# The attention rows x are written to DRAM from Pool's DMA queue instead of SyncE's

## The chip, the cores and the metric

The kernel runs on one core of a Trainium2 chip. The metric is device time in microseconds of one execution. Of the kernel before there are three timed runs (1334.05, 1337.35 and 1341.32 us, median 1337.35) and one execution taken with the hardware profiler (1334.38 us, of which 1332.6 us lie between the first and the last instruction).

## The reference

Three steps, all in float32, on 8 x 576 = 4608 tokens:

1. Chunked attention: q, k, v of 8 batches, 8 heads, 576 positions, 64 dimensions. In each chunk of 64 positions the softmax of the scaled scores weights v. The heads of a token are put side by side, so x has 4608 rows of 512.
2. A mixture of experts with a skip: tokens with x @ w_skip > 0 go to the one of 8 experts with the largest logit x @ w_gate, and get x + p * relu(x @ w1[e]) @ w2[e], where p is that expert's softmax weight. Other tokens keep x.
3. A dense layer: h = x @ w_in (512 to 2048), an activation made of three quadratic and linear pieces, and then @ w_out (back to 512).

## The kernel before, in words

**Tiling.** The 4608 tokens are cut into 18 units of 256 (UNIT, NU), each of two halves of 128. A unit's q, k and v are 512 KB each. The loop at line 849 is software-pipelined over units: iteration i transposes q and k of unit i+2 (s_T, e_T), loads q and k of unit i+4 and v of unit i+2 (load_qk, load_v), transposes the exponentials of unit i (s_ET), takes the scores of unit i+1 (s_SC), the weighted sum of unit i (s_AV), the transposes of x of unit i-1 (s_XT), the logits of unit i-2 (s_LG), its choice of expert (s_SEL), and the ranks of unit i-3 (s_RANK), which end in two scatters of token numbers into the experts' lists (f_put, line 578).

**The rows x.** s_AV writes a unit's rows into the tile xn: line 382 clears the last four columns on Pool, line 400 multiplies the sums by the reciprocals on VectorE, once for each half. The pool of xn has 4 buffers, so the tile of unit u is taken again by unit u+4. Some iterations later f_gate (line 497) puts the token's gate weight into column 512 with a reciprocal (line 500), and calls put_x, which writes the 256 rows of 516 floats to x_dram. For the last two units the columns 0 to 511 are written earlier, straight after s_AV (lines 876 and 902), and f_gate writes columns 512 to 515 alone.

**The order around the write.** All instructions of the attention part are issued in the order in which the program lists them (tc.manual_schedule). Small VectorE steps wait in the list `fill`; a call of dve() emits the next one between larger steps. The nine steps of s_SEL(u), f_gate the last of them, are emitted in iteration u+3, f_gate between the two halves of s_AV. In that iteration SyncE's queue has the loads of q and k (line 266, two to four DMAs), the eight loads of v (line 280), and then the write of unit u (line 507). Pool has the memset of line 382 and the two scatters. An engine takes its instructions in order, and a DMA that must wait for data holds back those behind it on the same engine.

**After attention.** The last iterations also load and split the weights of the first expert (piece; the low parts by VectorE or Pool, line 166) and run an early block of tokens (s_EARLY, b_X to b_M2). Then, from about 256 us, the experts, and from about 515 us the dense layer, which are bound by matmuls. Experts gather rows of x_dram by index, from Pool.

Of the kernel before, what the change touches and what calls it, by code (L numbers as in the profile page):

```python
# [86 lines left out]
def kernel(ctx, tc, q, k, v, w_skip, w_gate, w1, w2, w_in, w_out, consts, out):  # L87
    nc = tc.nc
# [363 lines left out]
    def e_SEL(us, b):  # L452
# [44 lines left out]
        def f_gate():  # L497
            T["gated", us[0]] = True
            for i, (u, xn) in enumerate(zip(us, xs)):
                nc.vector.reciprocal(out=xn[:, :, GATE:GATE + 1], in_=sm[:, 2 * i:2 * i + 2])  # L500
                put_x(u, xn, slice(DM if u + 2 >= NU else 0, ROW))
# [2 lines left out]

    def put_x(u, xn, cut):
        rows = x_dram[u * UNIT:(u + 1) * UNIT, cut].rearrange("(s p) c -> p s c", p=P)
        (nc.sync if cut.start == 0 else nc.scalar).dma_start(out=rows, in_=xn[:, :, cut])

    scat, hots = [], []

# [293 lines left out]
    with tc.manual_schedule():  # L804
# [44 lines left out]
        for i in range(NU - 1):  # L849
# [25 lines left out]
            if i + 2 == NU:  # L875
                put_x(i, T["x", i], slice(0, DM))
# [23 lines left out]
        run(b[:2])  # L900
        s_AV(u, 1)
        put_x(u, T["x", u], slice(0, DM))
        b_X()
        q = s_RANK(u - 3)
# [36 lines left out]
        for s in range(4):  # L941
# [3 lines left out]
            out=key, in0=cnt, scalar=float(NE), in1=cst[:, C_PREF - C_SEL:C_PREF - C_SEL + NE], op0=ALU.mult, op1=ALU.add  # L945
# [7 lines left out]
            out=perm, in0=cst[r24, C_POS - C_SEL:C_POS - C_SEL + NL], scalar=own[r24, 1:2], in1=cst[r24, C_BLK - C_SEL:C_BLK - C_SEL + NL], op0=ALU.is_equal, op1=ALU.mult  # L953
# [42 lines left out]
    with tc.If(total > 0):  # L996
        fb = tc.tile_pool(name="fb", bufs=1, reuse_waits="tile")
        with fb as f_p, tc.For_i(0, NE, 1) as j:
# [4 lines left out]
            with tc.For_i(0, n_j, 1) as b:  # L1003
# [8 lines left out]
                    out=fx, out_offset=None, in_=x_dram[:, :], in_offset=bass.IndirectOffsetOnAxis(ap=fi[:, 0:1], axis=0)  # L1012
# [5 lines left out]
                for h in range(4):  # L1018
                    w = f_p.tile([P, KD, 2 * P], F32, tag="fw", name="fw", bufs=3)
                    nc.sync.dma_start(  # L1020
                        out=w, in_=w1.rearrange("e (k p) f -> p (e k) f", p=P)[:, bass.ds(e * KD, KD), h * 2 * P:(h + 1) * 2 * P]
# [7 lines left out]
                for h in range(4):  # L1029
                    w = f_p.tile([P, 2, DM], F32, tag="fw", name="fw", bufs=3)  # L1030
                    nc.sync.dma_start(
                        out=w, in_=w2.rearrange("e (f p) d -> p (e f) d", p=P)[:, bass.ds(e * (F1 // P) + 2 * h, 2), :]
# [5 lines left out]
                    out=fx[:, 0:DM], in0=bk, scalar=fx[:, GATE:GATE + 1], in1=fx[:, 0:DM], op0=ALU.mult, op1=ALU.add  # L1038
                )
                nc.gpsimd.indirect_dma_start(  # L1040
                    out=x_dram[:, :],
                    out_offset=bass.IndirectOffsetOnAxis(ap=fi[:, 0:1], axis=0),
                    in_=fx,
# [238 lines left out]
```

## Time and profile before

| | |
|---|---|
| Median of the timed runs | 1337.35 us |
| The profiled execution: its time, its span | 1334.38 us, 1332.6 us |
| TensorE busy (matmuls) | 1252.7 us, 94% |
| VectorE, ScalarE, Pool busy | 678.6, 663.1, 216.5 us |
| DMA queue q1, issued by SyncE | 136.24 MB |
| DMA queue q10, issued by ScalarE | 46.75 MB |
| DMA queue q0, software, issued by Pool | 18.70 MB |

Busy time of TensorE is an average over stages. The page's second part shows the span in 40 slices of 33 us: each digit is the busy share of a slice in tenths, and PEclk the granted clock in tenths of full speed (2.4 GHz; the other level is 1.2). A wait is idle time of an engine just before an instruction, put down to what ended last by the profile. "issue" is time for which the profile shows no cause. In the list of DMA queues, the share is of the time of the core's 16 DMA engines.

### The profile page before, as it was taken

How to read it: one execution, taken by the hardware profiler on the slowest of the kernel's cores; microseconds unless marked ns; L12 is line 12 of the kernel's file. 1: busy time of each engine (PE TensorE's matmuls, PEld its weight loads, DVE VectorE, ACT ScalarE, POOL GpSimd, SP SyncE). 2: the span in 40 equal slices, each digit the busy share in tenths (PEclk: the TensorE clock that was granted, in tenths of full speed). 3: DMA queues.
4: the chain of work that ended last, by engine and by line, in shares of the span. 5: the costliest groups of instructions: out<-in, count | busy, mean ns of one | idle time of the engine just before them, and what ended most of it. 6: DMA issues, size and time to landing. Idle time of an engine off the chain costs nothing.

```text
span 1332.6 us, 19838 instructions
## 1 busy us (share of the span) xinstructions
PE 1252.7 (94%) x7127; PEld 1056.2 (79%) x7128; DVE 678.6 (51%) x1308; ACT 663.1 (50%) x1115; POOL 216.5 (16%) x259
## 2 busy tenths in 40 slices
PE   7877867889989999999999999999999999999998
PEld 6766856679878987888888888887888888888887
DVE  6645647647777675211221121001866686668665
ACT  7756645235544421222332232223776687668764
POOL 3011115532443444011111111000000000000000
PEclk9989888799999999999999999999999999999999
DMA  9879797267667666433543432234443343334431
GB/s 219 205 144 156 161 146 195 89 190 266 225 219 252 192 206 213 165 131 138 171 153 110 159 140 108 109 118 150 121 125 118 113 126 119 119 121 117 126 118 41
DMA packets 165371, 202.98 MB, mean 152 GB/s; under 512 B 51274, under 2 KB 88421, under 8 KB 165270
## 3 DMA queue, kind: packets, MB, share of 16 engines
q1 hardware_dynamic: 130966, 136.24, 38.1%
q10 hardware_dynamic: 26320, 46.75, 9.3%
q0 software_dynamic: 7984, 18.70, 4.4%
q8 instruction: 57, 0.93, 0.3%
q14 instruction: 44, 0.36, 0.1%
HBM read 135.88 MB, written 66.48 MB: 152 GB/s over the span
## 4 chain that ended last, share of the span: by engine, by line
PE 72%; DVE 3%; DMA 2%; issue 1%; ACT 0%; POOL 0%; SPq 0%; ACTq 0%; DVEq 0%; POOLq 0%
PE b L137 30%; PE a L137 29%; PE bank L137 6%; PE big L137 5%; PE t L140 1%; DMA stg<-in_moe_w_dram 1%; DVE a L192 1%; DVE a L191 1%; DMA stg<-in_moe_w_in_dram 0%; DVE s L193 0%; PE t L137 0%; PE big L687 0%; DVE hl L716 0%; DVE al L166 0%; DMA xs<-x_dram 0%
## 5 line engine op out<-in xcount | busy, mean ns | idle before, releaser
L137 PE MATMUL b<-bh,xh 128*128 128x512 f32 x576 | 226.0, 392 | 1.7 <-ACT xh L1181 1.7
L137 PE MATMUL b<-bh,xl 128*128 128x512 f32 x576 | 225.7, 392 | 0.0
L137 PE MATMUL b<-bl,xh 128*128 128x512 f32 x576 | 224.8, 390 | 0.0
L137 PE MATMUL a<-xh,ah 128*128 128x512 f32 (+1 forms) x576 | 223.9, 389 | 0.0
L137 PE MATMUL a<-xl,ah 128*128 128x512 f32 (+1 forms) x576 | 222.6, 386 | 0.4 <-DVE xl L1135 0.3
L137 PE MATMUL a<-xh,al 128*128 128x512 f32 (+1 forms) x576 | 222.5, 386 | 0.0
L1159 ACT COPY hs<-a 128x512 f32<-128x512 f32 x142 | 83.3, 587 | 275.6 <-PE a L137 264.9
L1182 DVE TENSOR_TENSOR xl<-r,xh 128x512 fp32r<-128x512 f32 x144 | 99.7, 692 | 108.7 <-ACT xh L1181 97.5
L1135 DVE TENSOR_TENSOR xl<-t,xh 128x512 fp32r<-128x512 f32 x34 | 22.0, 687 | 230.4 <-ACT xh L1134 230.3
L137 PEld LDWEIGHTS b<-bh,xh 128*128 128x128 f32 x576 | 108.4, 188 | 26.9 <-ACT xh L1181 5.0
L137 PEld LDWEIGHTS b<-bh,xl 128*128 128x128 f32 x576 | 108.5, 188 | 26.3 <-DVE xl L1182 3.9
L137 PEld LDWEIGHTS b<-bl,xh 128*128 128x128 f32 x576 | 108.6, 188 | 22.5
L137 PEld LDWEIGHTS a<-xl,ah 128*128 128x128 f32 x576 | 108.3, 188 | 22.0 <-DVE xl L1135 0.8
L137 PEld LDWEIGHTS a<-xh,al 128*128 128x128 f32 x576 | 108.2, 188 | 22.0
L137 PEld LDWEIGHTS a<-xh,ah 128*128 128x128 f32 x576 | 108.2, 188 | 21.5 <-ACT xh L1134 0.3
L1171 DVE SCALAR_TENSOR_TENSOR hs<-hs,r 128x512 f32<-128x512 f32 x144 | 99.7, 692 | 46.0 <-ACT r L1170 46.0
L1181 ACT CAST xh<-r 128x512 fp32r<-128x512 f32 x144 | 89.6, 622 | 53.3 <-PE b L137 34.5
L1175 ACT ACTIVATE hs<-hs,bias 128x512 f32<-128x512 f32 x144 | 104.2, 723 | 0.4 <-ACT hs L1159 0.4
L1170 ACT ACTIVATE r<-hs,bias 128x512 f32<-128x512 f32 x144 | 102.1, 709 | 0.5 <-ACT hs L1159 0.5
L1176 DVE TENSOR_TENSOR r<-r,hs 128x512 f32<-128x512 f32 x144 | 99.7, 693 | 2.6 <-ACT hs L1175 2.0
L326 ACT COPY qt<-big 64x512 f32<-64x512 f32 x72 | 44.7, 621 | 62.4 <-PE big L140 61.6
L140 PE MATMUL big<-ident,qu 128*128 128x128 f32 x144 | 26.8, 347 | 45.9 <-issue 40.2
(217 smaller groups left out, 2041.7 us busy)
## 6 DMA issues: line engine op xcount, KB each, us to landing
h_dram<-hs ACTq DMA_DIRECT2D x144, 256.0 KB
hs<-h_dram SPq DMA_DIRECT2D x144, 256.0 KB
stg<-in_moe_w_dram SPq DMA_DIRECT2D x128, 256.0 KB
vbd<-in_v_dram SPq DMA_DIRECT2D x144, 64.0 KB
xs<-x_dram SPq DMA_DIRECT2D x17, 512.0 KB
out_dram<-o ACTq DMA_DIRECT2D x34, 256.0 KB
x_dram<-xn SPq DMA_DIRECT2D x16, 516.0 KB
stg<-in_moe_w_in_dram SPq DMA_DIRECT2D x16, 512.0 KB
```

Source lines behind the costliest of these rows:

```text
L137: nc.tensor.matmul(out=o, lhsT=l, rhs=r, start=start, stop=stop)
L140: nc.tensor.transpose(out=o, in_=i, identity=ident)
L191: nc.vector.tensor_scalar(out=a, in0=top, scalar1=3, scalar2=0x3FFFFFFF, op0=ALU.logical_shift_left, op1=ALU.bitwise_and)
L326: (nc.vector.tensor_copy if eng is nc.vector else nc.scalar.copy)(out=o, in_=b4[64 * r:64 * r + 64, :, par, :])
L1135: nc.vector.tensor_tensor(out=xl[:, :, cut], in0=b3, in1=xh[:, :, cut], op=ALU.subtract)
L1159: nc.scalar.copy(out=hs, in_=b)
L1170: nc.scalar.activation(out=r, in_=h, func=ACTF.Relu, bias=bias[:, 0:1])
L1171: nc.vector.scalar_tensor_tensor(out=h, in0=h, scalar=-1.0, in1=r, op0=ALU.max, op1=ALU.subtract)
L1175: nc.scalar.activation(out=h, in_=h, func=ACTF.Square, scale=0.5, bias=bias[:, 1:2])
L1176: nc.vector.tensor_tensor(out=r, in0=r, in1=h, op=ALU.add)
L1181: nc.scalar.copy(out=gh, in_=r)
L1182: nc.vector.tensor_tensor(out=gl, in0=r, in1=gh, op=ALU.subtract)
```

## The change

put_x issues its DMA on Pool (nc.gpsimd) where it issued it on SyncE (nc.sync). The condition is not changed: it holds where the columns start at 0.

```
     def put_x(u, xn, cut):
         rows = x_dram[u * UNIT:(u + 1) * UNIT, cut].rearrange("(s p) c -> p s c", p=P)
-        (nc.sync if cut.start == 0 else nc.scalar).dma_start(out=rows, in_=xn[:, :, cut])
+        (nc.gpsimd if cut.start == 0 else nc.scalar).dma_start(out=rows, in_=xn[:, :, cut])
```

Its three calls:

```
put_x(u, xn, slice(DM if u + 2 >= NU else 0, ROW))   # f_gate, every unit
put_x(i, T["x", i], slice(0, DM))                    # line 876, i = NU - 2
put_x(u, T["x", u], slice(0, DM))                    # line 902, u = NU - 1
```

## Rows read from the trace of the kernel before

**Rows 1.** The page, parts 1 and 2: TensorE's busy time, and its slices.

```profile
PE 1252.7 (94%) x7127; PEld 1056.2 (79%) x7128; DVE 678.6 (51%) x1308; ACT 663.1 (50%) x1115; POOL 216.5 (16%) x259
...
PE   7877867889989999999999999999999999999998
```

**Rows 2.** Busy time by stretch: us, each engine, clock, DMA share, GB/s.

```profile
0.00:20.00 20.00, 13.21 (x120) 11.89 (x121) 11.23 (x17) 13.06 (x22) 11.77 (x31) 1.00 0.98 247
20.00:57.00 37.00, 35.55 (x455) 31.30 (x456) 26.38 (x73) 33.81 (x58) 0.00 (x0) 1.00 0.82 191
57.00:201.00 144.00, 103.17 (x1129) 92.97 (x1129) 71.35 (x274) 79.86 (x141) 20.85 (x31) 0.86 0.83 156
```

**Rows 3.** VectorE in order of time, lines 400 and 500: start, us, instruction, idle before.

```profile
39.60 0.69 DVE L400 TENSOR_TENSOR xn<-big,rc 128x512 f32<-128x512 f32 x1
...
48.46 0.69 DVE L400 TENSOR_TENSOR xn<-big,rc 128x512 f32<-128x512 f32 x1
...
106.10 0.16 DVE L500 RECIPROCAL xn<-sm 128x2 f32<-128x2 f32 x1
...
118.15 0.69 DVE L400 TENSOR_TENSOR xn<-big,rc 128x512 f32<-128x512 f32 x1 [3.49 <-DMA x_dram<-xn]
...
118.83 0.16 DVE L500 RECIPROCAL xn<-sm 128x2 f32<-128x2 f32 x1
...
134.82 0.69 DVE L400 TENSOR_TENSOR xn<-big,rc 128x512 f32<-128x512 f32 x1
...
145.86 0.69 DVE L400 TENSOR_TENSOR xn<-big,rc 128x512 f32<-128x512 f32 x1
...
201.18 0.69 DVE L400 TENSOR_TENSOR xn<-big,rc 128x512 f32<-128x512 f32 x1
```

**Rows 4.** Waits, 57 to 201 us: total us, times, longest.

```profile
POOL xn L382 <- DMA x_dram<-xn: 132.3, 10, 49.3
...
DVE xn L400 <- DMA x_dram<-xn: 41.1, 10, 6.0
PE big L140 <- issue: 40.2, 10, 6.0
```

**Rows 5.** SyncE's DMA issues in order of time.

```profile
33.25 0.55 SPq L266 DMA_DIRECT2D qu<-in_q_dram  x1
...
41.28 1.14 SPq L266 DMA_DIRECT2D qu<-in_q_dram  x2
...
109.63 0.55 SPq L507 DMA_DIRECT2D x_dram<-xn  x1
```

**Rows 6.** TensorE in order of time: eight transposes of q.

```profile
48.39 1.07 PE L140 MATMUL big<-ident,qu 128*128 128x128 f32 x8
...
134.57 1.94 PE L140 MATMUL big<-ident,qu 128*128 128x128 f32 x8 [5.44 <-issue]
```

**Rows 7.** DMA: the stretch 57 to 201 us, then the whole page's.

```profile
DMA packets 49028, 22.41 MB, mean 156 GB/s; under 512 B 25718, under 2 KB 46198, under 8 KB 49014
...
q0 software_dynamic: 640, 0.01, 0.4%
...
q0 software_dynamic: 7984, 18.70, 4.4%
...
x_dram<-xn SPq DMA_DIRECT2D x16, 516.0 KB
```

**Rows 8.** Pool: L207 by tile, L578 by line (57 to 201 us), L382 in time.

```profile
L207 POOL DMA_DIRECT2D m2w<-stg x8: 760/772/791, 321.1 to 461.7; - x8
...
L578 POOL DMA_INDIRECT idx_dram<-cst,si x20 | 19.7, 985 | 31.7 <-DVE acc L555 28.6 <-issue 3.0
...
118.19 0.10 POOL L382 MEMSET xn<- 128x8 f32 x1 [7.83 <-DMA x_dram<-xn]
```

**Rows 9.** Pool in order of time, in the tail of attention.

```profile
223.37 2.49 POOL L166 TENSOR_TENSOR al<-stg,ah 128x512 fp32r<-128x512 f32 x2 [4.43 <-ACT ah L164]
```

## The prediction

> **What bounds the kernel now.** I read the page first: TensorE is busy for 94% of the span [rows 1], so time can only come from slices in which it is not. Those are the first ten, up to the end of attention; from about 300 us on nearly every digit is 9. The view by stretches narrows it [rows 2]: from 20 to 57 us TensorE works 35.55 of 37 us at a granted clock of 1.00; from 57 to 201 us only 103.17 of 144 us, at a mean clock of 0.86, while ScalarE, VectorE and Pool have slack too (79.86, 71.35 and 20.85 us). The DMA engines show the same share in both stretches (0.82 and 0.83) but move 191 GB/s in the first and 156 GB/s in the second.
>
> What begins at 57 us? The second xn multiply of each unit (line 400) is a good clock for the loop [rows 3]. Unit 2 to unit 3 takes 48.46 - 39.60 = 8.86 us. From unit 3 (48.46) to unit 14 (201.18) there are eleven units in 152.7 us, 13.88 us each. The waits [rows 4] say why: VectorE stands 41.1 us in ten waits at line 400, Pool 132.3 us at the memset of line 382, both for the DMA x_dram<-xn. There are four xn buffers, so unit u+4 may not be written until the rows of unit u have left. TensorE's 40.2 us of "issue" in ten pieces are the same ten stalls one step on: its next transposes need a PSUM buffer that the multiply has not yet freed.
>
> The transfer itself is not long; it stands in a queue [rows 5]. Unit 4's gate is written at 106.10 [rows 3]. SyncE, which still issues loads of v, comes to the write at 109.63. Memset and multiply of unit 8 start at 118.19 and 118.15 [rows 3, 8]: freed 8.6 us after issue, 12.1 us after the gate. The next gate follows that multiply by 0.7 us (118.83) [rows 3], so the loop cannot be shorter than 12.1 + 0.7 = 12.8 us; from gate to gate this period was 118.83 - 106.10 = 12.7 us. So the write's lag is the loop's length.
>
> The eleven units add up: 8.86 of work x 11 = 97.5; waits 41.1; the remaining 14.1 us is mostly clock. After a stall eight transposes span 1.94 us where they otherwise span 1.07 [rows 6]; with 24 transposes a unit that is up to 3 x 0.87 = 2.6 us. Unit 10, which had no wait but began in this state, took 145.86 - 134.82 = 11.04 us [rows 3, 6].
>
> **The change part by part.** *Which writes move.* The condition is cut.start == 0. It is true also of the columns 0 to 511 of the last two units (lines 876 and 902), so all 18 large writes leave SyncE's queue, the 16 of 516 KB [rows 7] and those two; only the two small writes of the last units' gates stay on ScalarE's.
>
> *SyncE* loses 11 issues of about 0.55 us in the stretch, and more important, its loads are no longer issued behind a write, nor the write behind loads. Without writes it issued a unit's loads in 41.28 - 33.25 = 8.0 us [rows 5], which fits under 8.86.
>
> *Pool* gains 18 issues. A write of 512 KB from Pool took 0.77 us (L207, eight times); the two index scatters of a unit take 0.99 us each [rows 8]. Per unit Pool then has 0.77 + 2 x 0.99 + 0.10 = 2.9 us of a period of 9 to 14: hidden. In Pool's order the write stands after the unit's memset, and waits for the reciprocal of line 500. Behind it are the two scatters, whose index VectorE makes only after the gate, and the next unit's memset, which is not wanted before the next multiply. Nothing there is late by more than the 0.77 us.
>
> *The write's lag.* It would be issued at its gate, at 106.1 instead of 109.6. The trace of before shows no such write from Pool, so I bound issue-to-free: not below the 2.5 us or so that the bytes need at the highest rate of rows 2 (0.53 MB at 247 GB/s is 2.1, and some issue), not above today's 8.6 us unless Pool's queue is served worse (a rival below). With 8.6 the write allows a loop of 0.8 + 8.6 + 0.7 = 10.1 us, with 2.5 one of 4.0 us. Either way it is shorter than the next limit, so ten waits of 41.1 us go.
>
> *What is late next: the DMA engines.* In the stretch 22.41 MB move, 2.04 MB a unit [rows 7]. The bytes stay. From below: compute alone, 8.86 us a unit (it would need 230 GB/s; 247 were reached at the start). From above: today's 156 GB/s, 13.1 us. Between: 2.04 MB at the 191 GB/s of the undisturbed stretch is 10.7 us; and the time the engines are busy now, 0.83 x 13.1 = 10.9 us a unit, at the 0.98 share of the first stretch is 11.1 us [rows 2]. I take 11.0 us. Gain: 11 x (13.88 - 11.0) = 31.7 us. Bounds: 11 x (13.88 - 8.86) = 55 us, and 11 x (13.88 - 13.1) = 9 us.
>
> The Trainium skill, page "DMA: Bandwidth & Descriptors", section "Issuing engines are not separate DMA queues", says that DMAs from any issuing engine run on the same 16 DMA engines and that spreading them saves only issue time. By that rule alone the bytes would go no faster, and the time would be that of the first rival below. The rows agree as far as the equal share goes (0.82, 0.83), but the wait in rows 4 is for one write's place in line, not for bytes.
>
> *After 201 us.* Unit 15 (11.1 us, no wait) begins at the low clock and may gain 1 to 2 us. In the tail Pool splits weights (L166) between waits for ScalarE, one of 4.43 us [rows 9]. Five of the writes fall there (units 13 to 17): hidden in such waits they cost nothing, uncovered 5 x 0.77 = 3.9 us; I take 1.5. The two cancel. Everything from 256 us on shifts.
>
> **The sum** against the profiled execution: its own time is 1334.38 (span 1332.6). 1334.4 - 31.7 = 1302.7. The median before, 1337.35, lies 3.0 us above that execution: 1305.7, so I say **1305**.
>
> **Rivals.**
> *The DMA engines are full already (0.17).* The waits then turn into waits of the transposes for q and k, or of the matmuls of s_AV for v. For it: share 0.83 all through, and a rate that fell when the writes began. Against: a 17% rest, and ten waits that all name the write and none that name a load. At 13.1 us a unit the gain is 9 us, at 13.5 it is 4: about 1331.
> *Compute is the next limit (0.15).* For it: 247 GB/s in the first 20 us. Against: that stretch has no writes. 55 us: 1282.
> *Pool's queue serves the write worse (0.10): slower.* The place is the same wait at lines 382 and 400. It decides when gate-to-free plus 0.7 us exceeds 13.9, that is when issue-to-free exceeds 12.4 us instead of 8.6. At 14 us the loop is 15.5 us: 11 x 1.6 = 18 us more, 1355. For it: Pool has to generate this transfer itself and its queue moved only 0.01 MB in the stretch [rows 7]. Against: L578 beside the same VectorE work takes 0.99 us as everywhere.
> The Trainium skill, page "SBUF — State Buffer", section "SBUF: two separate sides", warns that a DMA issued from Pool stalls while a two-port VectorE instruction holds the shared port. By it the lag would grow by the length of such an instruction, 0.69 us if it is as long as line 400's, a fifth of what this rival needs; no row shows it.
> *The change does less than it says (0.03).* If only the writes inside the loop mattered and the last two units stayed, the result would differ by under 1.6 us: no case of its own.
>
> **How the numbers follow.** Forecast (10 to 12.5 us a unit, gain 15 to 43) 0.55; compute limit 0.15; engines full 0.17; slower 0.10; the rest 0.03. I put the eight-in-ten range from the compute limit to the engines-full case: 1281 to 1333. About 0.5% (6.7 us) is what a measurement of this kernel can tell from no change. Faster: 0.55 + 0.15 + 0.10 of the engines-full case + 0.01 of the rest = 0.81; same: 0.07 of the engines-full case + 0.01 of the slower one + 0.02 of the rest = 0.10; slower 0.09.
>
> **What would show it.** Right: line 400's wait for x_dram<-xn falls from 41.1 us to under 10; unit 14's second multiply comes near 170 instead of 201; clock of the stretch above 0.9; the software queue carries some 9.5 MB more than its 18.70; 18 Pool issues of line 507 near 0.8 us; after attention the same times, shifted. The DMA step is right if waits for qu, ku or vbd appear and units take 10 to 12 us; wrong if units take 9 us (then the engines were not the next limit) or stay at 13. The whole is wrong if line 382 still waits for x_dram<-xn as long as now.

## The result: faster by 1.4%, less than forecast

The changed kernel takes 1320.28 us in the median of four runs, the one before 1339.34 beside it: a ratio of 0.986, with a 95% interval of 0.982 to 0.990. The forecast was 1305 us, a gain of 32 us; the gain is 19 us, and 12.2 us between the two profiled executions (spans 1332.6 and 1320.4 us). The measured time lies inside the range of 1281 to 1333 us.

The profile after, busy time by stretch (us, then TensorE, its weight loads, VectorE, ScalarE and Pool, the granted clock, the DMA share and GB/s), is to be read against [rows 2]:

```profile
20.00:57.00 37.00, 33.33 (x432) 29.29 (x430) 25.05 (x68) 31.73 (x54) 0.88 (x2) 1.00 0.81 196
57.00:201.00 144.00, 115.01 (x1310) 101.23 (x1308) 86.34 (x327) 92.44 (x166) 36.22 (x49) 0.89 0.79 170
```

TensorE works 12 us more in the same 144 us, and the rate goes from 156 to 170 GB/s at a share of the DMA engines that is lower than before, 0.79 against 0.83. So the engines were not what filled up.

The waits of that stretch (total us, times, longest), against [rows 4]:

```profile
POOL xn L382 <- DMA x_dram<-xn: 25.4, 6, 10.1
...
PE big L137 <- DMA vbd<-in_v_dram: 11.5, 5, 4.8
...
PE big L140 <- DMA qu<-in_q_dram: 7.7, 3, 6.5
PE big L140 <- DMA ku<-in_k_dram: 7.0, 3, 4.4
...
DVE xn L400 <- DMA x_dram<-xn: 2.9, 2, 2.6
```

Line 400's wait for the row write falls from 41.1 to 2.9 us. In its place stand waits for loads: 11.5 + 7.7 + 7.0 = 26.2 us of TensorE. The first of these kinds, TensorE's wait for v, was not in the profile of before at all.

The second multiply of units 3, 14, 15 and 17 in the changed kernel, VectorE in order of time, against [rows 3]:

```profile
50.22 0.69 DVE L400 TENSOR_TENSOR xn<-big,rc 128x512 f32<-128x512 f32 x1
...
177.25 0.69 DVE L400 TENSOR_TENSOR xn<-big,rc 128x512 f32<-128x512 f32 x1
...
196.75 0.69 DVE L400 TENSOR_TENSOR xn<-big,rc 128x512 f32<-128x512 f32 x1
...
220.42 0.69 DVE L400 TENSOR_TENSOR xn<-big,rc 128x512 f32<-128x512 f32 x1
```

The kernel before had units 15 and 17 here:

```profile
212.30 0.69 DVE L400 TENSOR_TENSOR xn<-big,rc 128x512 f32<-128x512 f32 x1
...
235.02 0.69 DVE L400 TENSOR_TENSOR xn<-big,rc 128x512 f32<-128x512 f32 x1
```

Eleven units take 177.25 - 50.22 = 127.0 us, 11.55 each instead of 13.88. At unit 14 the changed kernel is 201.18 - 177.25 = 23.9 us ahead; at unit 15 only 15.6, at unit 17 14.6, at the end 12.2. A third of the gain is lost in one unit. There TensorE waits for the last load of q, which SyncE had issued 13.5 us earlier (SyncE's issue, then TensorE's transposes):

```profile
171.31 0.38 SPq L266 DMA_DIRECT2D qu<-in_q_dram  x1
```
```profile
184.82 1.94 PE L140 MATMUL big<-ident,qu 128*128 128x128 f32 x8 [6.55 <-DMA qu<-in_q_dram]
```

Pool's issues and its queue, against [rows 7, 8]: 18 writes at 0.76 us each, and 28.20 MB where there were 18.70.

```profile
L507 POOL DMA_DIRECT2D x_dram<-xn x18: 718/764/792, 50.3 to 233.0; - x18
```
```profile
q0 software_dynamic: 10576, 28.20, 6.4%
```

### The profile page after: what moved, and what is told of

It reads as the page before. It is cut to its first block, busy times and chain, and to the rows that moved or that the text cites. A ratio compares the mean times of both kernels' runs of the same rounds, so it can differ in the third digit from the quotient of the medians.

```text
span 1320.4 us, 19843 instructions
## 1 busy us (share of the span) xinstructions
PE 1244.3 (94%) x7126; PEld 1047.5 (79%) x7128; DVE 681.9 (52%) x1308; ACT 663.0 (50%) x1115; POOL 230.5 (17%) x277
## 3 DMA queue, kind: packets, MB, share of 16 engines
q0 software_dynamic: 10576, 28.20, 6.4%
## 4 chain that ended last, share of the span: by engine, by line
PE 74%; DVE 3%; DMA 1%; issue 1%; ACT 0%; SPq 0%; ACTq 0%; DVEq 0%
PE b L137 30%; PE a L137 29%; PE bank L137 6%; PE big L137 6%; PE t L140 1%; DVE a L192 1%; DVE a L191 1%; DMA stg<-in_moe_w_dram 1%; DMA stg<-in_moe_w_in_dram 1%; PE t L137 0%; PE big L687 0%; DVE s L193 0%; DVE al L166 0%; DMA xs<-x_dram 0%; PE spare L137 0%
## 5 line engine op out<-in xcount | busy, mean ns | idle before, releaser
L137 PEld LDWEIGHTS a<-xh,ah 128*128 128x128 f32 x576 | 108.2, 188 | 21.5 <-ACT xh L1134 0.3
L204 POOL TENSOR_TENSOR a<-a,bh 128x512 f32<-128x512 f32 x16 | 20.7, 1292 | 267.3 <-ACT bh L203 267.3
```

The costliest lines, as they stand in the source:

```text
L137: nc.tensor.matmul(out=o, lhsT=l, rhs=r, start=start, stop=stop)
L204: nc.gpsimd.tensor_tensor(out=af, in0=af, in1=hi, op=ALU.subtract)
```

## The experiments

My first theory: the row write's lag in SyncE's queue, against four buffers, was the loop's length, and any way of shortening it brings the gain. The first three runs undo or replace one part of that; the fourth looks at what stalls the loads. "us a unit" below is always from the second multiply of unit 3 to that of unit 14, divided by eleven, from one profiled execution. It says how long the loop is, not the whole time: in the profiles of runs 1, 2 and 9 the eleven units take 10.7, 12.9 and 14.7 us less than before, but unit 17 is then only 1.4, 8.7 and 4.3 us ahead. Each ratio is against runs of the kernel before beside that run.

**1. A fifth buffer, writes still on SyncE.**

```
-        et = e_p.tile([P, 2, HP, P], F32, tag="et", name="et")
+        et = e_p.tile([P, 2, HP, P], F32, tag="et", name="et", bufs=1)
...
-            T["x", u] = x_p.tile([P, 2, ROW], F32, tag="xn", name="xn", bufs=4)
+            T["x", u] = x_p.tile([P, 2, ROW], F32, tag="xn", name="xn", bufs=5)
```

> The kernel before, its writes still on SyncE, with a fifth xn buffer (paid for by one et buffer instead of two). My theory (the wait is one write's lag in SyncE's queue against four buffers): the unit u+5 instead of u+4 waits for the write, so the wait of line 400 for x_dram<-xn falls from 41 us to under 8, and the time falls by about as much as with Pool's queue, 12 to 20 us. Rival (the queue itself matters, because loads behind a write are held up): the wait goes but waits for q, k and v take its place, gain under 6 us.

Ratio 0.998 (0.996 to 1.001): no gain, at 12.91 us a unit. Its waits, 57 to 201 us:

```profile
DVE xn L400 <- DMA x_dram<-xn: 19.8, 7, 5.7
PE big L140 <- DMA qu<-in_q_dram: 10.4, 4, 5.2
PE big L140 <- DMA ku<-in_k_dram: 6.1, 4, 2.2
PE big L137 <- DMA vbd<-in_v_dram: 5.0, 4, 2.1
```

The wait for the write is halved, and 21.5 us of waits for loads take its place. This is the rival's outcome: the loop gets shorter, the time does not. What the single et buffer costs by itself no run shows.

**2. The writes on ScalarE's queue.**

```
-        (nc.sync if cut.start == 0 else nc.scalar).dma_start(out=rows, in_=xn[:, :, cut])
+        nc.scalar.dma_start(out=rows, in_=xn[:, :, cut])
```

> All writes of x on ScalarE's queue instead of Pool's. My theory (any queue apart from the loads does it): within 5 us of the changed kernel, some 15 us under the one before; line 400's wait for x_dram<-xn under 8 us. Rival (there is something in Pool's software queue, good or bad): more than 8 us off the changed kernel, either way.

Ratio 0.999 (0.998 to 1.001), 12.71 us a unit. Line 400 waits for no write any more, but v is late:

```profile
PE big L137 <- DMA vbd<-in_v_dram: 18.4, 10, 3.7
```

My theory falls here: a queue apart from the loads is not enough. Nor is a place ahead of the scatters, which the write has here too: ScalarE issues it at 107.36, the scatters of the unit before follow at 109.17 (below). And ScalarE is hardly held up by its new work: its instruction behind the write waits 2.0 us in all for VectorE.

```profile
107.36 0.37 ACTq L507 DMA_DIRECT2D x_dram<-xn  x1
```
```profile
ACT xt L418 <- DVE sl L562: 2.0, 2, 1.2
```

The Trainium skill, page "DMA: Bandwidth & Descriptors", section "Issuing engines are not separate DMA queues", says that another issuing engine saves only issue time. This run agrees with it (0.999), the changed kernel (0.986) does not.

The same run shows what the loads wait for. Pool issues two index scatters:

```profile
109.17 0.98 POOL L578 DMA_INDIRECT idx_dram<-cst,si  x1 [6.53 <-DVE acc L555]
110.45 0.98 POOL L578 DMA_INDIRECT idx_dram<-cst,si  x1 [0.30 <-issue]
```

and this is what all DMA moves around them, in stretches of 2 us (the last two columns are the DMA share and GB/s):

```profile
109.00:111.00 2.00, 1.03 (x5) 1.06 (x6) 0.33 (x3) 0.00 (x0) 1.53 (x2) 0.70 1.16 334
111.00:113.00 2.00, 2.00 (x12) 1.94 (x11) 0.00 (x0) 0.99 (x2) 0.43 (x1) 0.50 1.05 258
113.00:115.00 2.00, 2.00 (x21) 1.42 (x21) 0.61 (x1) 1.95 (x4) 0.00 (x0) 0.95 0.30 29
115.00:117.00 2.00, 2.00 (x34) 1.79 (x32) 1.34 (x6) 1.95 (x5) 0.10 (x1) 1.00 0.27 15
117.00:119.00 2.00, 1.27 (x17) 1.02 (x16) 2.00 (x8) 1.75 (x5) 0.00 (x0) 1.00 0.12 26
119.00:121.00 2.00, 0.00 (x0) 0.00 (x0) 0.94 (x4) 0.48 (x1) 0.00 (x0) 1.00 0.28 49
```

For 8 us next to nothing moves, 15 to 49 GB/s, though loads of v are queued, and the DMA engines are mostly without a packet (a share of 0.12 to 0.30). This is the longest such stretch of the run's loop. In others the share stays high while the rate falls (1.25 at 42 GB/s in the changed kernel, shown further down).

**3. The loads listed behind the write, on SyncE.**

```
-            load_qk(i + 4)
-            load_v(i + 2)
             s_ET(i)
...
             s_AV(i, 1)
+            load_qk(i + 4)
+            load_v(i + 2)
```

> The writes stay on SyncE, but each unit's loads are listed behind the unit's write instead of ahead of it. My theory (place in line): the write is issued within 1 us of its gate where SyncE is not late, the lag falls from 12 us to 6 to 9, the wait of 41 us to under 20, the time by 5 to 15 us. Rival (a write ahead of loads in one queue costs the loads what it saves itself): no change within 5 us.

Ratio 0.997 (0.994 to 0.999), 13.44 us a unit; line 400 still waits 25.9 us for the write. A place ahead in line takes 15 us off that wait and hardly shows in the time: no change within 5 us, as the rival had it.

**4. The changed kernel without the scatters of units 0 to 11.**

```
         def f_put():
+            if u < NU - LATE:
+                return
```

> The changed kernel without the index scatters of units 0 to 11 (left out; the lists of these units stay at their first values, so the tokens gathered are other ones). In the changed kernel the loads stall after about 65 us: slices of 1 us fall to 29 to 70 GB/s with the engines busy. Theory A (the stalls come from the scattered 4-byte index writes): the stalls go, units take 9 to 9.5 us instead of 11.5, unit 14 ends near 155 instead of 177, the time falls by another 15 to 25 us. Theory B (they come from the row writes beside loads): the time stays within 5 us of the changed kernel.

1284.59 us, ratio 0.965 (0.961 to 0.968) against the kernel before. Its stretch:

```profile
57.00:201.00 144.00, 128.37 (x1525) 109.42 (x1523) 107.42 (x408) 103.50 (x191) 36.36 (x50) 0.94 0.77 211
```

211 GB/s at a smaller share than before the change, and 8.95 us a unit, close to the 8.86 that [rows 3] show for compute alone. This is theory A: the scatters cost the stretch nearly everything above compute.

**5. As many small writes, 64 bytes apart.** far_dram is a tensor of its own that nothing reads.

```
+    far_dram = tc.dram_tile([(NE * NT + P) * 16, 1], F32, name="far_dram")
...
-            ... scalar1=FAR, scalar2=None, op0=ALU.add)
+            ... scalar1=FAR, scalar2=float(16), op0=ALU.add, op1=ALU.mult)
...
-                    out=idx_dram[:, :],
+                    out=far_dram[:, :],
...
-                    bounds_check=NE * NT - 1,
+                    bounds_check=(NE * NT - 1) * 16,
```

> The changed kernel with each scattered index written to a slot 64 bytes from the next instead of 4 (in a tensor of its own that nobody reads, so the lists keep their first values and other tokens are gathered, as in the run without scatters). As many 4-byte writes as before. Theory A1 (the stall comes from many small writes close together in memory): stalls mostly go, unit 14 under 155 us, time within 8 us of the run without scatters (1285). Theory A2 (each small write costs the same wherever it lands): time within 6 us of the changed kernel (about 1320).

1278.13 us, ratio 0.960 (0.955 to 0.966); 8.98 us a unit:

```profile
57.00:201.00 144.00, 128.89 (x1532) 109.83 (x1531) 109.86 (x412) 104.45 (x192) 60.97 (x74) 0.93 0.78 212
```

So it is not the number of the small writes but how close they lie: in the kernel before, neighbouring tokens of one expert take neighbouring slots, 4 bytes apart. The page "DMA: Bandwidth & Descriptors" of the Trainium skill, section "Specifications", says that below 512 bytes the DMA reads, modifies and writes. That would hold at either distance; the runs show that with 64 bytes between them the same writes cost the loop nothing that can be seen.

**6. The slots 16 bytes apart, read and used.** The lists are four times as long, set by four DMAs, and read with a stride (excerpts):

```
-    idx_dram = tc.dram_tile([NE * NT + P, 1], F32, name="idx_dram")
+    idx_dram = tc.dram_tile([(NE * NT + P) * 4, 1], F32, name="idx_dram")
+    idx_w = idx_dram.rearrange("(n w) o -> n (w o)", w=4)
...
-        il = dec_p.tile([NL, P], F32, tag="a", name="il")
+        il = dec_p.tile([NL, P * 4], F32, tag="a", name="il")
...
-        mm(bk[:, 0:NL], il, perm)
+        mm(bk[:, 0:NL], il.rearrange("b (p w) -> b p w", w=4)[:, :, 0], perm)
```

> The changed kernel with list slots 16 bytes apart, read and used (four times the bytes to set and to read the lists). By A1 a part of the stalls goes: 1295 to 1315. By A2: 1320 to 1326, a little above the changed kernel for the longer first setting of the lists.

1283.25 us, ratio 0.964 (0.958 to 0.969): better than I expected by 12 us, and better than both kernels of this study. 9.14 us a unit. In the 2 us stretches around two of its scatters (issued at 95.89 and 97.20) the rate does not break down; the lowest is 131 GB/s:

```profile
97.00:99.00 2.00, 2.00 (x28) 1.42 (x28) 0.94 (x3) 1.95 (x4) 1.09 (x2) 1.00 0.82 174
99.00:101.00 2.00, 2.00 (x38) 1.76 (x34) 1.49 (x5) 1.95 (x5) 0.00 (x0) 1.00 0.94 223
101.00:103.00 2.00, 2.00 (x31) 1.82 (x28) 2.00 (x9) 1.95 (x5) 0.00 (x0) 1.00 0.99 280
103.00:105.00 2.00, 1.73 (x20) 1.49 (x18) 2.00 (x8) 1.21 (x3) 0.76 (x1) 1.00 0.58 131
```

The same holds on the mean. Over the 8 us from the second scatter of each pair on, DMA moves 100 to 224 GB/s in the kernel before, 110 to 190 in the changed one, 78 to 165 in run 2, but 193 to 233 in this run and 209 to 237 in run 5 (pairs issued between 57 and 190 us; in runs 5 and 6 the ten issued up to 150 us).

**7. Pool's queue, but the scatters ahead of the write.** f_gate only notes the unit for units 1 to 11, and the write is listed behind the two scatters of the unit before:

```
-                put_x(u, xn, slice(DM if u + 2 >= NU else 0, ROW))
+                if u + 2 >= NU or u < 1 or u >= NU - 6:
+                    put_x(u, xn, slice(DM if u + 2 >= NU else 0, ROW))
+                else:
+                    T['put', u] = xn
...
-            return [f_slot, lambda: [f_si(), f_put()]]
+            def late_put():
+                if ('put', u + 1) in T:
+                    put_x(u + 1, T.pop(('put', u + 1)), slice(0, ROW))
...
+            return [f_slot, lambda: [f_si(), f_put(), late_put()]]
```

> The changed kernel, but for units 1 to 11 the row write is listed behind the two index scatters of the unit before instead of ahead of them, both on Pool. Writing on ScalarE's queue gained nothing, writing on Pool's did. Theory P1 (on Pool the scatters queue behind the row write and so are spread out in time): the gain is lost, 1328 to 1335. Theory P2 (the gain is in how Pool's queue moves the rows themselves, two rows in one packet): no change, 1316 to 1324.

1340.15 us, ratio 1.005 (1.002 to 1.008): the whole gain is gone. One unit, the gate on VectorE and then Pool in order of time:

```profile
112.82 0.15 DVE L500 RECIPROCAL xn<-sm 128x2 f32<-128x2 f32 x1
```
```profile
116.13 0.99 POOL L581 DMA_INDIRECT idx_dram<-cst,si  x1 [0.30 <-issue]
117.09 0.79 POOL L510 DMA_DIRECT2D x_dram<-xn  x1
128.33 0.10 POOL L382 MEMSET xn<- 128x8 f32 x1 [10.45 <-DMA x_dram<-xn]
```

The write is issued within 1 us of the second scatter, and its buffer is free 11.2 us later, against 8.6 us in the unit of before that the prediction reads; line 400 waits 43.7 us in all. In the changed kernel the same write, on the same queue, stands ahead of the scatters. So on Pool's queue the gain hangs on which of the two comes first. Behind the scatters it also goes out later, 4.3 us after its gate instead of 0.5; the run does not price the two parts one by one.

**8. The kernel before without the scatters of units 0 to 11.**

```
         def f_put():
+            if u < NU - LATE:
+                return
```

> The kernel before (writes on SyncE) without the index scatters of units 0 to 11 (left out as in the earlier run). If the write's long lag is itself made by the stalls: waits of line 400 for x_dram<-xn under 5 us and the time within 4 us of the changed kernel without scatters (1285). If the place in SyncE's queue makes a lag of its own: at least 10 us above it, 1295 or more.

1287.62 us, ratio 0.968 (0.961 to 0.974). In time it is the first of the two outcomes expected: 3 us above the changed kernel without scatters, which the intervals cannot tell apart. But line 400 still waits 11.8 us for the write, not under 5, and a unit takes 10.07 us against 8.95. SyncE's queue makes a lag of its own that is worth 12 us at unit 14; little of it reaches the end.

**9. ScalarE's queue, the scatters held until the write has landed.**

```
-        (nc.sync if cut.start == 0 else nc.scalar).dma_start(out=rows, in_=xn[:, :, cut])
+        T['write'] = nc.scalar.dma_start(out=rows, in_=xn[:, :, cut]).ins
...
+                if u < NU - LATE:
+                    tc.add_manual_dep(ins.ins, T["write"].name, SYNC, reason="experiment")
```

> The writes on ScalarE's queue, as in the run that gained nothing, and each unit's two scatters now wait until the row write issued just before them has landed, as Pool's own queue made them nearly do in the changed kernel. Theory P1 (the gain comes from the scatters starting behind the row write): 1316 to 1326, near the changed kernel. If something else of Pool's queue matters, no change from the earlier run: 1328 to 1336.

Ratio 1.002 (1.000 to 1.003), 12.54 us a unit: no gain. Holding the scatters behind the write is not enough by itself.

**10 and 11. Slots 16 bytes apart, with the writes on SyncE and on Pool.** The first is experiment 6 with put_x as in the kernel before; the second is experiment 6 again.

> The kernel before, writes on SyncE, with list slots 16 bytes apart. If the change only helped against the stalls of the scatters: within 5 us of the same slots with Pool's writes (1283), with a rest of waits of line 400 for x_dram<-xn (some 12 us, as without scatters). If the queue is worth something by itself: 8 us or more above it.

> The changed kernel with list slots 16 bytes apart once more, beside the same with SyncE's writes on one chip: 1280 to 1287.

1301.98 us and 1286.21 us, beside 1328.74 of the kernel before: ratios 0.979 (0.977 to 0.981) and 0.968 (0.966 to 0.971). With slots 16 bytes apart Pool's queue is worth 15.8 us, the second outcome expected (8 us or more). With no scatters at all in the loop (runs 4 and 8) it was 3 us, which the intervals cannot tell from nothing; why the two differ no run shows. On SyncE a unit takes 10.87 us, and the old wait is back in small:

```profile
DVE xn L401 <- DMA x_dram<-xn: 15.5, 9, 4.6
```

On Pool it is 9.03 us a unit and that wait is not in the list.

**12. The writes of units 12 to 17 back on SyncE.**

```
-        (nc.gpsimd if cut.start == 0 else nc.scalar)
+        ((nc.gpsimd if u < NU - LATE else nc.sync) if cut.start == 0 else nc.scalar)
```

> The changed kernel with the writes of units 12 to 17 back on SyncE's queue. By my term for the tail (Pool's six issues there cost up to 3.9 us): 1316 to 1320, at most 4 us faster. If the tail's writes gain from Pool's queue too: slower, 1322 to 1328.

1310.03 us where the kernel before took 1328.74: a ratio of 0.986 (0.984 to 0.989), the same as the change's own. The kernel before was 10 us faster beside this run than beside the change, so the numbers of us that I expected don't apply; the ratios show that the tail's writes neither cost nor bring anything that can be measured. In its profile unit 15 takes 11.4 us, not the 19.5 of the changed kernel, but unit 10 takes 15.3 and unit 16 17.1: where the stalls fall differs from execution to execution.

## Why the prediction was right in direction and too large

- **The ten waits go: right.** 41.1 us became 2.9 us, for the reason given: the write leaves 0.5 us after its gate. Two of the signs named fell a little short: unit 14 came at 177.25 instead of near 170, and the clock of the stretch rose to 0.89, not above 0.9.
- **"The transfer itself is not long; it stands in a queue": half right.** Of the 12.1 us from gate to free buffer, 3.5 were the place in line and 8.6 the transfer. Without scatters on the same queue (run 8; gate at 89.81) it is 4.9 us in line and 4.5 us of transfer, so about half of the transfer's time was the scatters' stall:

```profile
94.72 0.55 SPq L507 DMA_DIRECT2D x_dram<-xn  x1
```
```profile
99.17 0.10 POOL L382 MEMSET xn<- 128x8 f32 x1 [9.90 <-DMA x_dram<-xn]
```

- **Pool has room: right.** 0.76 us an issue; I had 0.77 from another transfer of the same size. No sign that VectorE's work held the issues up (longest 0.79 us).
- **"What is late next: the DMA engines", 11.0 us a unit: near in size (11.55), wrong in cause.** I took the engines' busy share for work that must be done. Runs 4 and 5 show that with the same row writes and loads a unit takes 9 us at 211 GB/s, so neither bytes nor engines set 11. The bound is the stall behind each unit's two scatters; it was in the profile of before (shown below), hidden in a mean of 156 GB/s over 144 us. I had weighed that mean and the clock, but no stretch of a few us. The sign named for this step, waits for loads and 10 to 12 us a unit, came true all the same: it could not tell a stall from full engines. The nearness of 11.0 to 11.55 is luck, the more so as a slip lies in the sum: 2.04 MB a unit and the 13.1 us of "today's" rate divide a stretch of 144 us by eleven units, though at 13.88 us it holds 10.4. Divided rightly it is 2.16 MB, the two estimates between the bounds are 11.3 and 11.8 us, and the lower bound of a 9 us gain falls away, since today's rate gives today's 13.88. The eleven units bring 25.7 us instead of 31.7; unit 3 itself was 1.8 us late.
- **"The two cancel. Everything from 256 us on shifts": the step that failed most.** Unit 15, which was to gain 1 to 2 us, lost 8.4, because the load of q for unit 17 took 13.5 us from issue to use. Two scatters were issued at 178.90 and 180.21, and DMA moved 115 and 90 GB/s in the next two stretches of 2 us, from 179 to 183 us: it looks like the same stall. Without these scatters (run 4) unit 15 takes 10.4 us; with them it took 11.4 in run 12, so not every pair costs this much. Another 3.4 us went between unit 15 and the end. So 23.9 us became 12.2 in the profiled pair. The Pool term of the tail was not to blame (run 12), though it was counted wrong: six writes fall there (units 12 to 17), not five.
- **The rival "engines are full already"** named the waits that came (q, k and v) and the wrong reason. **"Pool's queue serves the write worse"** did not happen, but its place was right: run 7 frees the buffer 11.2 us after the write's issue, the same two lines wait, and the kernel is 0.5% slower than before. The price of 1355 us was not reached. **"Compute is the next limit"**, 8.86 us a unit and 1282 us, is what came once the slots lay apart (run 6: 9.14 us a unit, 1283 us).

What the runs show of the change's own mechanism: in the kernel before, SyncE comes to the row write when Pool has already issued the two scatters of the unit before. The rate breaks down behind them, and the buffer is free 10.3 us after the issue (the scatters, the write, two stretches of 2 us, the memset that waited):

```profile
158.51 0.97 POOL L578 DMA_INDIRECT idx_dram<-cst,si  x1 [2.53 <-DVE acc L555]
159.79 0.98 POOL L578 DMA_INDIRECT idx_dram<-cst,si  x1 [0.30 <-issue]
```
```profile
161.76 0.55 SPq L507 DMA_DIRECT2D x_dram<-xn  x1
```
```profile
161.00:163.00 2.00, 2.00 (x35) 1.55 (x36) 1.19 (x4) 1.76 (x4) 0.00 (x0) 1.00 0.15 32
163.00:165.00 2.00, 2.00 (x42) 2.00 (x39) 2.00 (x7) 1.93 (x5) 0.00 (x0) 1.00 0.25 25
```
```profile
172.08 0.10 POOL L382 MEMSET xn<- 128x8 f32 x1 [11.31 <-DMA x_dram<-xn]
```

On Pool the write goes out at its gate, about 1.5 us ahead of the scatters. Of the six row writes for which a memset still waits in the stretch, four free their buffer 5.2 to 7.0 us after issue, but two only after 11.2 and 13.9 us. The one of 11.2 us, with the rate behind it:

```profile
141.19 0.76 POOL L507 DMA_DIRECT2D x_dram<-xn  x1 [3.84 <-DVE sl L562]
142.73 1.00 POOL L578 DMA_INDIRECT idx_dram<-cst,si  x1 [0.78 <-DVE acc L555]
144.04 0.99 POOL L578 DMA_INDIRECT idx_dram<-cst,si  x1 [0.30 <-issue]
...
152.38 0.10 POOL L382 MEMSET xn<- 128x8 f32 x1 [7.35 <-DMA x_dram<-xn]
```
```profile
147.00:149.00 2.00, 1.24 (x24) 0.99 (x18) 2.00 (x7) 1.93 (x5) 0.00 (x0) 1.00 1.25 42
```

So the head start gets most writes through ahead of the stall, not all of them, and it leaves the loads in the stall. Run 7 takes the head start away and loses everything.

What stays open: runs 1 and 2 show that taking line 400's wait away brings no time by itself, so what turns it into a gain on Pool's queue is shown only as far as the order of run 7. Nor is it known why the same write on ScalarE's queue, which has the head start too, with the scatters held back behind it or not (runs 9 and 2), leaves 12.5 to 12.7 us a unit where Pool's queue leaves 11.55. In both line 400's wait is gone; in run 2 TensorE waits more for v, 18.4 us against 11.5, in run 9 less, 7.1. No run separates the queues' service of the loads from the form in which each moves the rows: the 9.5 MB of rows are 2592 packets on Pool's queue and 4896 on ScalarE's. A fifth buffer with Pool's writes was not run.

## What to carry to other kernels

When a wait on one transfer is removed, ask what every other transfer waits for at that moment: look at the DMA rate in stretches of 2 us, not of 33, before calling the engines the next limit. A rate that breaks down while loads are queued points at another transfer, and a small one can do it. Of scattered writes of a few bytes, try spacing the destinations before moving anything else: here that alone was worth 27 us (run 10, ratio 0.979), the change alone 19 us (0.986), both together 42.5 us (run 11, 0.968).

## What the runs showed of the hardware that was not expected

Two scatters of 128 four-byte writes each, to slots 4 bytes apart, left all DMA at 15 to 49 GB/s for 8 us in the deepest case (run 2), and at 78 to 165 GB/s on the mean of 8 us behind the ten pairs. At 16 bytes apart that mean was 193 to 233 GB/s (run 6; the lowest single 2 us up to 151 us had 84), and at 64 bytes a unit took 8.98 us, as with no scatter at all (8.95). By what means close writes hold the others up no run shows.
